# Scores on two row tiles of 64x128 in place of four 64x64 tiles

## The chip, the cores and the metric

The kernel runs on one core of a Trainium2 chip. The metric is the device time of that core in microseconds (us). Times of several runs are given by their median; a trace comes from one profiled execution.

## What is computed

A chunked linear attention with decay, followed by a mixture of experts with one expert for each token. There are 4 batches, 8 heads, 768 positions and a head size of 64; 3072 tokens of width 512; 8 experts with 1024 hidden units. Cut to what matters:

```
for each block of the sequence, for each batch and head:
    scores = (q_block @ k_block.T) * decay_mask        # lam ** (i - j), 0 above the diagonal
    out    = scores @ v_block + (q_block * lam ** (i + 1)) @ kv_state
    kv_state = lam ** block * kv_state + (k_block * rev_decay).T @ v_block
x = attention output, one row of 512 for each token
expert  = argmax(x @ w_gate + modality_bias);  gate = softmax value of that expert
result  = gate * (relu(x @ w1[expert]) @ w2[expert])
```

## The kernel before

Two stages follow one another. The attention stage works on 24 chunks of 128 positions (6 for each of 4 batches, `g` from 0 to 23), each with all 8 heads. Heads go in pairs: of the 128 partitions a pair's first head has 0 to 63 and its second 64 to 127. The second stage multiplies tiles of up to 256 tokens, gathered by expert, with that expert's weights in fp32r.

TensorE can be used as one array of 128 rows by 128 columns, or as several smaller tiles (64x64, 128x64 and so on) that stand in different rows or columns of it. The rows are those of the operands' partitions, the columns those of the output's partitions; the profile shows the shape in use for each group as "64*64", "128*64", "128*128". All attention matmuls are plain fp32.

One turn of the chunk loop (lines 721 to 775) gives TensorE, in this order:

- `scores(g)`, line 204: for each of 4 head pairs and each head (`hl`, its 64 partitions are the slice `r`), keys times queries, in two halves `s` of the 128 key positions. Each matmul has 64 rows (the head size), 64 weight columns (64 keys) and streams 128 queries: four 64x64 tiles, 16 matmuls for a chunk. The two heads write two PSUM tiles `s` of one bank each (chunk 1 uses a tile `x` for the second). VectorE multiplies each with the decay mask into `pt` (line 207).
- `from_state(g - 1)`, line 242: the carried state times decayed queries, on 64x64 tiles, into PSUM tiles `o`. It is left out for the first chunk of a batch.
- `outputs(g - 1)`, line 253: values times `pt` of the chunk before, on two 128x64 column tiles, added to the same `o`; ScalarE copies `o` to `xt` (line 255).
- `carry(g)`, line 219: what the chunk adds to the state, on two 128x64 column tiles; left out for the last chunk of a batch.
- `tokens(g - 2)`, line 266: turns `xt` to rows of tokens and adds the gate's logits, on two 128x64 column tiles.

The matmuls that rank the tokens for their experts (lines 321 to 326 and 360, 128x128) stand among these at a few places. SyncE's queue loads the chunks, 1 MB each, up to 6 ahead (line 73); ScalarE's queue writes the tokens out (line 270). The tile framework orders each engine's instructions by the program and adds the waits.

In the second stage line 572 transposes gathered tokens, and lines 579, 582 and 583 are the three fp32r products.

Of the kernel before, what the change touches and what calls it, by code (L numbers as in the profile page):

```python
# [37 lines left out]
def linear_attention_moe(tc, qkv, lam, modality, wg, mbias, w1, w2, out):  # L38
    nc = tc.nc
    with ExitStack() as ctx:  # L40
# [118 lines left out]
        halves2 = [slice(hl * D, (hl + 1) * D) for hl in range(2)]  # L159
# [8 lines left out]
        def loaded(g):  # L168

            t = chunks[g]  # L170
            kt, qt = (t[:, 0, i].rearrange("p (a t) -> p a t", a=NP) for i in range(2))
            return kt, qt, t[:, 1, 0], t[:, 1, 1]
# [23 lines left out]
        def scores(g):  # L196
            kt, qt, vt, kn = loaded(g)
            pts = []
            sps = [ps.tile([P, NP, P], F32, name="s", bufs=3),
                   ps.tile([P, NP, P], F32, name="x", bufs=2) if g == 1 else ps.tile([P, NP, P], F32, name="s", bufs=3)]  # L200
            for p in range(NP):
                for hl, r in enumerate(halves2):
                    for s in halves2:
                        nc.tensor.matmul(sps[hl][s, p, :], kt[r, p, s], qt[r, p, :], start=True, stop=True)  # L204
            for hl in range(2):
                pt = work.tile([P, NP, P], F32, name="pt", bufs=4)
                op = nc.vector.tensor_tensor(out=pt, in0=sps[hl], in1=dk[:, hl], op=ALU.mult)  # L207
                pts.append(pt)
            return pts, op
# [511 lines left out]
        for g in range(0, ng + 2):  # L721
            if g == 2:
                routing_constants()
            if g < ng:
                st1[g], masked = scores(g)
# [59 lines left out]
        hl = [work.tile([P, 2, TT], F32R, name=f"hl{i}", tag=t, bufs=3) for i, t in enumerate(("qd", "qd", "kd", "kd"))]  # L785
# [149 lines left out]
```

## Time and profile before

| | us |
|---|---|
| median of 3 runs | 414.44 (411.96 to 415.23) |
| profiled execution | 410.95 |
| its span, first to last instruction | 409.2 |
| TensorE busy with matmuls | 392.8 (96% of the span) |
| VectorE busy | 248.5 (61%) |
| ScalarE busy | 190.6 (47%) |
| GpSimd busy | 101.4 (25%) |

The profile has PE for TensorE's matmuls and PEld for its weight loads, which overlap them; DVE is VectorE, ACT ScalarE, POOL GpSimd, SP SyncE; a q behind an engine is its DMA queue. L204 is line 204. Matmuls are pipelined: one's busy time reaches into the next one's, so the pace of a group is read from starts, not from durations. The attention stage lies at about 6 to 108 us.

### The profile page before, as it was taken

Reading aid. Unit: us, or ns where it says so; the run is one execution under the profiler, and the core shown is the slowest. Engines: PE = TensorE matmul, PEld = TensorE weight load, DVE = VectorE, ACT = ScalarE, POOL = GpSimd, SP = SyncE. Lnnn points to the kernel's source line nnn. Section 1 sums busy time; section 2 is a strip of 40 time slices with the busy share of each in tenths; the row PEclk is TensorE's granted clock in tenths of the full one; section 3 lists DMA queues with packets and bytes.
Section 4 is the critical chain, followed back from the end, with each engine's and each line's share of the span. In section 5 each row is a group of like instructions: output and inputs, shape, how many; then the busy total and the mean of one; then the engine's idle time right before and its main releaser. Section 6 shows DMA issues by size and latency. Waiting matters only on the chain.

```text
span 409.2 us, 10757 instructions
## 1 busy us (share of the span) xinstructions
PE 392.8 (96%) x4224; PEld 347.7 (85%) x4224; DVE 248.5 (61%) x480; ACT 190.6 (47%) x345; POOL 101.4 (25%) x118
## 2 busy tenths in 40 slices
PE   8998989999799999999999999999999999999994
PEld 4877878888598987698999989898999989898983
DVE  6958849888489850378390918456381918366240
ACT  1333434443586231466463818274463818274330
POOL 4301323514513651041331210203021210200001
PEclk9999999999999999999999999999999999999999
DMA  7999979888820168010316586501111010200101
GB/s 284 408 384 409 352 277 343 284 293 286 314 79 3 53 192 332 11 54 1 105 50 217 172 276 203 185 33 51 53 51 54 23 55 26 70 28 7 48 1 48
DMA packets 24603, 62.58 MB, mean 153 GB/s; under 512 B 7645, under 2 KB 8157, under 8 KB 24544
## 3 DMA queue, kind: packets, MB, share of 16 engines
q1 hardware_dynamic: 15792, 42.81, 29.9%
q0 software_dynamic: 4768, 12.69, 9.3%
q10 hardware_dynamic: 3984, 6.31, 4.2%
q8 instruction: 35, 0.57, 0.5%
q14 instruction: 24, 0.20, 0.2%
HBM read 90.46 MB, written 13.67 MB: 254 GB/s over the span
## 4 chain that ended last, share of the span: by engine, by line
issue 45%; PE 26%; DMA 10%; POOL 7%; DVE 3%; POOLq 3%; SPq 3%; ACT 1%; DVEq 0%
PE s L204 6%; PE o L253 6%; PE x L266 6%; DMA idx<-inv 5%; POOL out_dram L657 4%; DMA xg<-xs,idx 4%; POOL xg L539 3%; POOLq L837 3%; PE o L242 2%; PE kv L219 2%; DMA load<-in_qkv_dram 2%; SPq L556 1%; DVE w1l L512 1%; PE s L583 1%; PE s L582 1%
## 5 line engine op out<-in xcount | busy, mean ns | idle before, releaser
L579 PE MATMUL s<-xh,w1h 128*128 128x256 f32 x384 | 107.4, 280 | 0.8 <-ACT xh L511 0.8
L583 PE MATMUL s<-xh,w1l 128*128 128x256 f32 x384 | 107.3, 280 | 0.5 <-DVE w1l L512 0.4
L582 PE MATMUL s<-xl,w1h 128*128 128x256 f32 x384 | 107.2, 279 | 0.0
L512 DVE TENSOR_TENSOR w1l<-raw,w1h 128x1024 fp32r<-128x1024 f32 x48 | 58.1, 1221 | 72.6 <-ACT w1h L511 72.6
L579 PE MATMUL o<-w2h,hh 128*128 128x512 f32 x192 | 75.8, 395 | 0.0
L583 PE MATMUL o<-w2h,hl 128*128 128x512 f32 x192 | 74.9, 390 | 0.0
L582 PE MATMUL o<-w2l,hh 128*128 128x512 f32 x192 | 74.8, 390 | 0.0
L579 PEld LDWEIGHTS s<-xh,w1h 128*128 128x128 f32 x384 | 72.2, 188 | 1.8 <-ACT xh L511 1.0
L583 PEld LDWEIGHTS s<-xh,w1l 128*128 128x128 f32 x384 | 72.2, 188 | 0.9 <-DVE w1l L512 0.9
L582 PEld LDWEIGHTS s<-xl,w1h 128*128 128x128 f32 x384 | 72.2, 188 | 0.6 <-issue 0.2
L512 DVE TENSOR_TENSOR w2l<-raw,w2h 128x1024 fp32r<-128x1024 f32 x48 | 58.5, 1220 | 2.1 <-ACT w2h L511 2.0
L511 ACT CAST w1h<-raw 128x1024 fp32r<-128x1024 f32 x48 | 49.8, 1055 | 20.4 <-PE s L582 19.7
L511 ACT CAST w2h<-raw 128x1024 fp32r<-128x1024 f32 x48 | 50.1, 1046 | 0.0
L656 ACT ACTIVATE y<-o,idx 128x512 f32<-128x512 f32 x20 | 13.8, 689 | 76.0 <-PE o L583 45.6
L657 POOL DMA_INDIRECT out_dram<-y,idx x20 | 20.3, 1013 | 115.5 <-ACT y L656 94.8
L598 DVE SCALAR_TENSOR_TENSOR hl<-s,hh 128x512 fp32r<-128x512 f32 x48 | 33.0, 688 | 21.6 <-ACT hh L597 21.5
L539 POOL DMA_INDIRECT xg<-xs,idx x20 | 25.3, 1264 | 73.6 <-PE x L572 68.0
L255 ACT COPY xt<-o 128x256 f32<-128x256 f32 x48 | 17.7, 373 | 54.0 <-PE o L253 49.1
L583 PEld LDWEIGHTS o<-w2h,hl 128*128 128x128 f32 x192 | 36.0, 188 | 7.5
L582 PEld LDWEIGHTS o<-w2l,hh 128*128 128x128 f32 x192 | 36.1, 188 | 7.2
L579 PEld LDWEIGHTS o<-w2h,hh 128*128 128x128 f32 x192 | 36.1, 188 | 7.1
L207 DVE TENSOR_TENSOR pt<-s,dk 128x512 f32<-128x512 f32 x47 | 30.1, 679 | 16.9 <-PE s L204 16.8
(185 smaller groups left out, 485.8 us busy)
## 6 DMA issues: line engine op xcount, KB each, us to landing
raw<-in_w_dram SPq DMA_DIRECT2D x104, 512.0 KB
load<-in_qkv_dram SPq DMA_DIRECT2D x22, 1024.0 KB
xs<-xn ACTq DMA_DIRECT2D x24, 256.0 KB
load<-in_qkv_dram SPq DMA_DIRECT2D x4, 512.0 KB
spare<-in_w_dram SPq DMA_DIRECT2D x4, 512.0 KB
w1h<-in_w_dram SPq DMA_DIRECT2D x4, 512.0 KB
inv<-pad SPq DMA_DIRECT2D x2, 196.0 KB
inv<-pad SPq DMA_DIRECT2D x2, 192.0 KB
```

What stands on the lines that cost most here:

```text
L204: nc.tensor.matmul(sps[hl][s, p, :], kt[r, p, s], qt[r, p, :], start=True, stop=True)
L207: op = nc.vector.tensor_tensor(out=pt, in0=sps[hl], in1=dk[:, hl], op=ALU.mult)
L253: mm = nc.tensor.matmul(op[half][place(p, hl), i, :], vt[:, (2 * p + hl) * D : (2 * p + hl + 1) * D], pts[hl][:, p, :], start=(c == 0 and ...
L266: nc.tensor.matmul(xp[r, j, : P + E], xt[:, p, r], iw[:, p, :], start=True, stop=True)
L511: cp = nc.scalar.copy(out=hi, in_=src)
L512: df = nc.vector.tensor_tensor(out=lo, in0=src, in1=hi.bitcast(F32), op=ALU.subtract)
L539: last = nc.gpsimd.indirect_dma_start(out=(to or xg)[t][:m], out_offset=None, in_=xs[:rows, :], in_offset=bass.IndirectOffsetOnAxis(ap=idx ...
L579: mm = nc.tensor.matmul(out, ah, bh, start=first, stop=False)
L582: nc.tensor.matmul(out, ah, bl, start=False, stop=False)
L583: return nc.tensor.matmul(out, al, bh, start=False, stop=last)
L598: nc.vector.scalar_tensor_tensor(out=hl[i], in0=hp, scalar=0.0, in1=hh[i].bitcast(F32), op0=ALU.max, op1=ALU.subtract)
L657: sc = nc.gpsimd.indirect_dma_start(out=out, out_offset=bass.IndirectOffsetOnAxis(ap=idx[:, t, 0:1], axis=0), in_=y, in_offset=None, bound ...
```

## The change

The four 64x64 tiles of the scores become two row tiles of 64x128: one matmul takes all 128 keys of a head as its 128 weight columns. There are 8 matmuls for a chunk in place of 16, each with the same 64 rows and 128 streamed queries. The PSUM tiles, what is written into them, and all other lines stay.

```diff
@@ -200,8 +200,7 @@
             for p in range(NP):
                 for hl, r in enumerate(halves2):
-                    for s in halves2:
-                        nc.tensor.matmul(sps[hl][s, p, :], kt[r, p, s], qt[r, p, :], start=True, stop=True)
+                    nc.tensor.matmul(sps[hl][:, p, :], kt[r, p, :], qt[r, p, :], start=True, stop=True)
             for hl in range(2):
```

## Rows read from the trace of the kernel before

**Rows 1.** Stretches: length; busy time (count) by engine; granted clock, DMA share, GB/s.

```profile
11.70:51.00 39.30, 37.36 (x863) 32.56 (x865) 32.26 (x82) 14.64 (x54) 7.00 (x11) 1.00 1.01 387
...
115.00:409.00 294.00, 287.36 (x1983) 258.59 (x1981) 162.60 (x244) 146.54 (x193) 62.73 (x54) 1.00 0.26 85
```

**Rows 2.** Chain of waits, 11.7 to 108.3 us, shares of that window by line.

```profile
by line: PE s L204 26.3%; PE o L253 25.0%; PE x L266 22.3%; PE o L242 9.8%; PE kv L219 9.3%; issue 5.9%; PE x L321 0.4%; ACT xn L268 0.4%; PE x L326 0.3%; PE x L360 0.1%; PE x L324 0.1%; ACT xe L269 0.1%
```

**Rows 3.** Groups by shape: tile, operands, count; busy us, mean ns; idle before.

```profile
L204 PE MATMUL s<-load 64*64 64x128 f32 x752 | 29.7, 277 | 2.9 <-issue 2.1 <-DMA load<-in_qkv_dram 0.8
...
L242 PE MATMUL o<-qd,state 64*64 64x128 f32 x320 | 14.0, 271 | 0.2 <-issue 0.2
```

**Rows 4.** TensorE in order of time: start us, length us, group, count; clean chunks.

```profile
60.46 1.10 PE L204 MATMUL s<-load 64*64 64x128 f32 x32
61.49 1.09 PE L253 MATMUL o<-pt,load 128*64 128x128 f32 x16
62.41 0.64 PE L219 MATMUL kv<-load,kd 128*64 128x64 f32 x16
62.88 1.10 PE L266 MATMUL x<-iw,xt 128*64 128x136 f32 x16
63.91 1.10 PE L204 MATMUL s<-load 64*64 64x128 f32 x32
64.83 0.62 PE L242 MATMUL o<-qd,state 64*64 64x128 f32 x16
65.38 1.09 PE L253 MATMUL o<-pt,load 128*64 128x128 f32 x16
66.30 0.63 PE L219 MATMUL kv<-load,kd 128*64 128x64 f32 x16
```

**Rows 5.** TensorE in order of time, the last chunk, which has no scores.

```profile
105.63 0.67 PE L242 MATMUL o<-qd,state 64*64 64x128 f32 x16
106.23 1.09 PE L253 MATMUL o<-pt,load 128*64 128x128 f32 x16
```

**Rows 6.** TensorE in order of time: transposes (one, then three), fp32r matmuls.

```profile
108.34 0.33 PE L572 MATMUL x<-ident,xg 128*128 128x128 f32 x1
...
108.34 0.55 PE L572 MATMUL x<-ident,xg 128*128 128x128 f32 x3
...
113.27 0.39 PE L579 MATMUL s<-xh,w1h 128*128 128x256 f32 x1
113.49 0.28 PE L582 MATMUL s<-xl,w1h 128*128 128x256 f32 x1
113.61 0.28 PE L583 MATMUL s<-xh,w1l 128*128 128x256 f32 x1
```

**Rows 7.** TensorE in order of time: first and last of seven gapped bursts.

```profile
26.11 0.66 PE L253 MATMUL o<-pt,load 128*64 128x128 f32 x8
27.50 0.66 PE L253 MATMUL o<-pt,load 128*64 128x128 f32 x8 [0.73 <-issue]
27.99 1.10 PE L266 MATMUL x<-iw,xt 128*64 128x136 f32 x16
...
102.05 0.62 PE L242 MATMUL o<-qd,state 64*64 64x128 f32 x16
103.68 1.09 PE L253 MATMUL o<-pt,load 128*64 128x128 f32 x16 [1.01 <-issue]
```

**Rows 8.** Stretches of about 256 TensorE instructions, columns as in the first group.

```profile
33.55:39.96 6.41, 5.45 (x127) 4.67 (x127) 5.43 (x13) 1.64 (x6) 0.94 (x2) 1.00 1.04 408
...
45.40:53.37 7.97, 6.05 (x128) 5.07 (x126) 4.89 (x14) 2.53 (x10) 2.77 (x3) 1.00 0.94 323
53.37:58.53 5.16, 5.16 (x126) 4.63 (x128) 2.83 (x6) 1.64 (x6) 0.96 (x1) 1.00 0.53 195
...
64.08:69.33 5.25, 5.04 (x135) 4.44 (x131) 4.63 (x14) 2.03 (x8) 2.71 (x4) 1.00 0.96 307
```

**Rows 9.** The page: busy time and instructions of engines; DMA queue of instructions: packets, MB, share.

```profile
PE 392.8 (96%) x4224; PEld 347.7 (85%) x4224; DVE 248.5 (61%) x480; ACT 190.6 (47%) x345; POOL 101.4 (25%) x118
...
q8 instruction: 35, 0.57, 0.5%
```

## What was predicted, before the change was run

> **What bounds the kernel now.** I read the stretches first [rows 1]. From 11.7 to 51 us TensorE is busy for 37.4 of 39.3 us with the DMA share at 1.01; from 115 us on it is busy for 287 of 294 us. So TensorE sets the pace in both stages, and a microsecond taken from or given to its attention stage should arrive at the end nearly whole. The chain of waits over 11.7 to 108.3 us says the same [rows 2]: the five groups of attention matmuls hold 93% of it, 5.9% is "issue" (TensorE waits for nothing that the profile shows), and no DMA or VectorE work holds 1%. So I looked for two things only: how long TensorE's bursts are, and where those issue gaps come from.
>
> The bursts are regular [rows 4]; I read them from the start of one burst to the start of the next. A chunk with a carried state is scores 0.92 us (63.91 to 64.83), state part 0.55 (64.83 to 65.38), outputs 0.92 (65.38 to 66.30), carry 0.47 (as 62.41 to 62.88), tokens 1.03 (62.88 to 63.91): 3.89 us.
>
> What does a score burst consist of? The trace shows each fp32 matmul as two, so the 16 of a chunk stand as 32 [rows 4]. The granted clock is 1.00 in both stretches, the 2.4 GHz level [rows 1], so durations compare. A lone pass of 128 columns with the whole array as one tile takes 0.11 us: three transposes last 0.22 us longer than one [rows 6]. The outputs, on two column tiles, do 16 passes in 0.92 us; the scores, on four tiles, do 32 in the same 0.92 us [rows 4]. So four passes run side by side in the scores: eight rounds of 0.109 us make 0.87, and 0.05 stays for the first weight load.
>
> **The change, part by part.**
>
> *Passes.* Half as many passes run two at a time: 16 on two row tiles are again eight rounds, 0.87 us. The row halves already run side by side in four tiles, so I price the streaming at nothing gained, nothing lost. No row shows 64x128 tiles side by side; if they ran one after the other it would be 16 rounds, a rival below.
>
> *A new change of shape.* Now scores and state part share 64x64, and the state part follows without a break. When another shape follows the scores, as in a batch's first chunk (60.46 to 61.49), the burst takes 1.03 in place of 0.92: 0.11 to change. A state part that follows another shape takes 0.60 (105.63 to 106.23 [rows 5]) and not 0.55: its first weight load is no longer hidden, 0.05. So 0.16 us for each score burst followed by a state part. There are 320/16 = 20 state bursts [rows 3], of which the one at 105.63 already follows other work: 19 x 0.16 = 3.0 us. The changes tokens to scores (128x64 to 64x64 now, 128x64 to 64x128 then) and state part to outputs exist on both sides. Bounds: 0 if 64x128 to 64x64 were no change of shape, 3.0 if it is one. Every row with a change of row or column size pays, so I take 3.0.
>
> The Trainium skill, "TensorEngine Tiling (Array Packing)", section "Tiling Modes", says that changing the tiling mode, other than changing the tile within it, drains TensorE. The trace agrees where 64x64 turns into 128x64 (0.11 us); by this rule the new change pays too, and the term stays 3.0.
>
> *Wider weight loads.* A score weight grows from 64 to 128 columns. The load ahead of the first round is exposed. Lower bound: 0.05, as for 64 columns. Upper bound: an fp32r matmul with 128 weight columns takes 0.22 us first in its burst and 0.12 after (113.27 to 113.49 to 113.61 [rows 6]), so 0.10. It is the nearest row, four-byte data of the same width: I take 0.10, 0.05 more for 24 bursts, 1.2 us (bounds 0 and 1.2).
>
> In steady rounds the load must hide behind one pass of the same 128 columns. The carry has that ratio, 64 weight columns to 64 streamed ones: eight rounds in 0.47 us are 0.058 each, against 0.0545 for half of 0.109. That is 0.004 a round: 24 x 8 x 0.004 = 0.8 us. Lower bound 0; upper bound from the fp32r row (0.117 by its steady step of 0.12, 0.008 over 0.109): 1.5 us.
>
> Added: 3.0 + 1.2 + 0.8 = 5.0 us, bounds 3.0 and 5.7.
>
> *Fewer instructions.* Seven bursts hold an issue gap. The first [rows 7] takes 1.88 us in place of 0.92 (26.11 to 27.99), the last 1.63 in place of 0.55 (102.05 to 103.68). By such differences the seven, in order, lose 0.96, 0.64, 1.19, 2.3, 0.54, 0.89 and 1.08 us, 7.6 in all. What are they waiting for? I cut the stage at the ends of the gaps, and between them where a count of about 256 falls, and counted TensorE's matmuls and weight loads [rows 8]: 254, 254, 254 and 266 in the windows shown (a window also counts what runs across its edges), between 252 and 271 in all 15 from 16 to 103.7 us. The seven gaps stand at the ends of such windows. So the gaps fall on a grid of about 256 instructions. The queue of kind "instruction" [rows 9] carries 35 packets, 0.57 MB, so 16 KB each, and TensorE has 4224 matmuls and 4224 loads [rows 9]: 241 for each packet. I conclude that TensorE's instructions come in packets of 256 and that it sometimes runs dry because the next one is late behind the data transfers: the DMA share is 1.04, 0.94 and 0.96 in the stalled windows shown, and 0.53 in one that has no gap.
>
> In a stalled window TensorE used up its packet and waited, so the window's length is how long the next packet took: 5.25 us at the shortest, 6.41 and 7.97 at the longest. A packet now lasts 256/192 x 3.89 = 5.2 us without a gap, since a chunk has 2 x (32+16+16+16+16) = 192 instructions. After the change a chunk has 160 and takes 3.89 + 0.16 + 0.05 + 0.03 = 4.13 us: 256/160 x 4.13 = 6.6 us. Six of the seven late packets would then be in time, and the slowest leaves 1.4 us: 7.6 - 1.4 = 6.2 us gained. This assumes that a packet is asked for about when the previous one is begun. If it is asked for halfway, only 0.7 of the 1.4 us more counts, and 0.3 + 0.5 + 1.6 + 0.2 + 0.4 = 3.0 stays: 4.6 gained. Bounds 0 (a rival) and 7.6; I take 6.2.
>
> The Trainium skill, "Runtime: NRT & Kernel Launch", section "Instruction fetch mechanics", says that instructions are refilled in blocks of 256 and that crossing a block is mostly hidden. The block size agrees with the windows, the hiding doesn't (up to 2.3 us lost at one). By the page's word on hiding the gaps would be something else, and fewer instructions would gain nothing: the sum would be 5.0 us slower.
>
> *Other engines.* The products with the decays (L207) still wait for the last score pass of the chunk, which ends where it did; no wait is added and no tile or buffer changes. The input chunks aren't on the chain, so a slightly faster or slower TensorE meets them in time.
>
> *Sum.* +5.0 - 6.2 = -1.2 us. Against the profiled execution (410.95 us, of which the span is 409.2) that is 409.8. The median of the runs shown, 414.44, lies 3.5 above the profiled one; on it the forecast is 413.2, rounded 413. The three runs spread over 3.3 us; if late packets cause that spread the gain is larger, which I leave to the range.
>
> **Rivals.**
>
> *Nothing is saved* (the other side). The gaps stay, because they don't come from the number of instructions, or because the packets take longer by as much. For it: that packets are asked for early is inferred. Against it: the grid of 256 that the gaps keep to. The page's "mostly hidden", of the Trainium skill's "Runtime: NRT & Kernel Launch" above, would make it this case. Price +5.0 (3.0 to 5.7): 419.4 us (417.4 to 420.1). It decides from a saving under 0.9 us on: then the change is slower by over 1% with the added work at 5.0.
>
> *The row tiles run one after the other.* 24 bursts x 8 rounds x 0.109 = 21 us more; the longer bursts leave time for all late packets, -7.6, and 5.0 stays: +18, 433 us. For it: no row has this shape in pairs, and a load of the full width might block the other tile. Against it: with four tiles, loads and passes of both row halves overlap fully.
>
> *The new shape change is free or the wider loads are*, and the packets come in time: added work 0 to 2 us, gain 6.2 or more (also where other runs stall more than the profiled one did): -4.2 to -7.6, about 409 us. Against it: every shape change in the rows pays its 0.1.
>
> **Chances.** My sum, with its own range -4.6 to +1.1 us (added 3.0 to 5.7, gained 4.6 to 7.6, so 410 to 415.5): 0.6. Nothing saved: 0.17. One after the other: 0.07. Free or larger gain: 0.16. About 1%, 4.1 us, is what a measurement of this kernel can tell from no change: faster takes the last case and the edge of mine, 0.19; slower takes 0.07 and most of the 0.17, 0.19; the same is 0.62. The range reaches to 420 to take in the second case and down to 408.5 into the last; it leaves out the serial tiles and the largest gains.
>
> **What would show it.** In the new trace the scores should stand as 384 matmuls on 64*128; scores to state part about 1.1 us and state part to outputs 0.60; the instruction queue some 32 packets; issue gaps on TensorE with one or two left, so that issue on the chain from 11.7 us on falls under 2%. A state part that still follows in 0.92 refutes the shape term; a burst of 1.9 us means serial tiles; issue gaps of 5 us or more in sum refute the saving.

## The result, and the profile after

| | before | after |
|---|---|---|
| median of 4 runs, us | 414.59 (411.96 to 415.23) | 407.57 (407.28 to 408.68) |
| ratio after to before | | 0.9864, 95% interval 0.9824 to 0.9903 |
| span of the profiled execution, us | 409.2 | 405.9 |
| first scores of chunk 2 to first transposes (L572, L571 after), us | 96.61 | 92.74 |
| start of the first transposes to start of the last matmul, us | 294.59 | 294.79 |

By the medians the changed kernel is 7.0 us (1.7%) faster; by the ratio in the table, which isn't the quotient of the two medians, it is 1.4%. The forecast was 413.0, and 407.6 lies 0.9 us below the low end of the range. The second stage is the same within 0.2 us. The two profiled executions (410.95 and 407.58 us) differ by 3.4 us: the attention stage gained 3.87, and a later start of chunk 2 (12.05 us in place of 11.73) and the second stage took 0.5 of it back. The other 3.6 us of the medians' difference come from the executions of before that weren't profiled, and they are a part of the story.

The page of the kernel after, which answers to [rows 9], and its group of score matmuls, which answers to the first of [rows 3] (tile shape, operands, count; busy us, mean ns; idle before):

```profile
PE 395.4 (97%) x3840; PEld 349.8 (86%) x3840; DVE 248.6 (61%) x480; ACT 190.6 (47%) x345; POOL 99.4 (24%) x118
...
q8 instruction: 32, 0.52, 0.5%
...
L203 PE MATMUL s<-load 64*128 64x128 f32 x376 | 30.1, 286 | 0.7 <-DMA load<-in_qkv_dram 0.7
```

TensorE has 384 matmuls and 384 weight loads fewer, and the queue of instructions three packets fewer. The scores' group is busy for 30.1 us, where it had 29.7, and has no idle time that ended by "issue"; before it had 2.1 us of it.

The chain of waits of the kernel after, 12.05 to 80 us, and then that of the kernel before from 11.7 to 80 us, shares by line:

```profile
by line: PE s L203 29.5%; PE o L252 24.8%; PE x L265 21.9%; PE o L241 13.2%; PE kv L218 9.8%; PE x L320 0.4%; PE x L325 0.3%; PE x L359 0.2%; PE x L323 0.1%; issue 0.1%
```

```profile
by line: PE s L204 27.6%; PE o L253 24.7%; PE x L266 21.3%; PE o L242 9.8%; PE kv L219 9.7%; issue 6.0%; PE x L321 0.4%; PE x L326 0.3%; PE x L360 0.2%; PE x L324 0.1%
```

"Issue" has gone from 6.0% to 0.1%. The scores and the state part (L241) have grown, from 37% to 43% of a shorter chain. So the change took away idle time that was nobody's work, and paid for it with longer bursts.

The bursts, in the timeline of TensorE after (start us, length us, group, count), to be read against [rows 4]:

```profile
63.77 1.10 PE L265 MATMUL x<-iw,xt 128*64 128x136 f32 x16
64.80 1.16 PE L203 MATMUL s<-load 64*128 64x128 f32 x16
65.89 0.67 PE L241 MATMUL o<-qd,state 64*64 64x128 f32 x16
66.49 1.09 PE L252 MATMUL o<-pt,load 128*64 128x128 f32 x16
67.41 0.64 PE L218 MATMUL kv<-load,kd 128*64 128x64 f32 x16
```

From start to start the scores take 1.09 us (64.80 to 65.89) where they took 0.92, the state part 0.60 (to 66.49) where it took 0.55. Outputs (0.92), carry (0.47) and tokens (1.03) are as they were. Of the score burst itself the first round, with its exposed weight load, takes 0.213 us where it took 0.160, and a later round 0.112 where it took 0.109.

The stretches of after, with busy time (count) by engine, granted clock, DMA share and GB/s, answer to [rows 1]:

```profile
12.05:51.00 38.95, 38.95 (x743) 34.31 (x743) 32.48 (x83) 14.85 (x55) 7.33 (x11) 1.00 1.02 395
...
112.00:406.00 294.00, 287.01 (x1978) 258.24 (x1977) 162.37 (x242) 145.96 (x193) 61.61 (x54) 1.00 0.26 85
```

TensorE is busy for all 38.95 us of the first stretch, beside a DMA share as high as before.

### The profile page after: what moved, and what is told of

It is laid out like the page before. It is cut to its first block, busy times and chain, and to the rows that moved or that the text cites. A ratio compares the mean times of both kernels' runs of the same rounds, so it can differ in the third digit from the quotient of the medians.

```text
span 405.9 us, 9991 instructions
## 1 busy us (share of the span) xinstructions
PE 395.4 (97%) x3840; PEld 349.8 (86%) x3840; DVE 248.6 (61%) x480; ACT 190.6 (47%) x345; POOL 99.4 (24%) x118
## 3 DMA queue, kind: packets, MB, share of 16 engines
q1 hardware_dynamic: 15792, 42.81, 30.1%
## 4 chain that ended last, share of the span: by engine, by line
issue 44%; PE 20%; DMA 16%; POOL 8%; DVE 3%; SPq 3%; POOLq 3%; ACT 0%; DVEq 0%
PE s L203 5%; DMA load<-in_qkv_dram 5%; DMA idx<-inv 4%; PE o L252 4%; POOL out_dram L656 4%; PE x L265 4%; DMA raw<-in_w_dram 4%; DMA xg<-xs,idx 4%; POOL xg L538 3%; POOLq L836 3%; PE o L241 2%; PE kv L218 2%; SPq L555 1%; DVE w1l L511 1%; PE s L582 1%
## 5 line engine op out<-in xcount | busy, mean ns | idle before, releaser
L538 POOL DMA_INDIRECT xg<-xs,idx x20 | 24.0, 1202 | 73.4 <-PE x L571 68.0
L206 DVE TENSOR_TENSOR pt<-s,dk 128x512 f32<-128x512 f32 x47 | 30.1, 679 | 14.0 <-PE s L203 14.0
```

The source lines that it names most:

```text
L538: last = nc.gpsimd.indirect_dma_start(out=(to or xg)[t][:m], out_offset=None, in_=xs[:rows, :], in_offset=bass.IndirectOffsetOnAxis(ap=idx ...
```

## The experiments

The theory: TensorE's instructions arrive in packets of 256; while the chunks are being loaded a packet takes 5 to 8 us, and TensorE runs dry when it uses one up sooner. Fewer instructions for each chunk make a packet last longer. The first rival: the gaps have to do with 64x64 tiles, and a shape that has none of them in the scores has no gaps. The second: the gaps come and go with the execution, and the after that was seen was a lucky one.

"Time of a packet" below is 256 divided by TensorE's instructions for a chunk, times the time of a chunk without gaps. A gap is counted from start to next start of TensorE's matmuls and loads, less what such a step usually takes; it is "on the grid" if it falls within one instruction of every 256th. Counted so, the seven gaps of the profile before are 6.6 us. (The prediction counted whole bursts and had 7.6: each restart costs about 0.14 us more, for a weight load that is exposed again.)

### The kernel before a second time

No edit.

> The kernel before, unchanged, with a second profile. If the spread of its runs (412 to 415 us) comes from late instruction packets, this profile shows issue gaps at the same grid of 256 TensorE instructions but of another sum than 7.6 us, and its span differs from 409.2 us by about the difference of the sums. If the spread comes from elsewhere, the sum stays near 7.6 us and the stretch after 108 us differs.

Measured: 414.51 us, 3.6 above the execution profiled first; in the other runs of before that went with it the median was 412.19. The stage takes 98.63 us (12.18 to 110.81) where it took 96.61. The chain of waits of this execution, 12.2 to 110.8 us, by line:

```profile
by line: PE s L204 25.9%; PE o L253 24.5%; PE x L266 21.9%; PE o L242 9.7%; PE kv L219 9.1%; issue 7.8%; ACT xn L268 0.4%; PE x L321 0.4%; PE x L326 0.3%; PE x L360 0.1%; ACT xe L269 0.1%; PE x L324 0.1%
```

Issue is 7.8% where [rows 2] had 5.9%: ten gaps on the grid, 8.9 us. One of them, in the timeline of TensorE, begins within the same burst as the first of [rows 7] and is longer (1.56 us in place of 0.73):

```profile
26.62 0.66 PE L253 MATMUL o<-pt,load 128*64 128x128 f32 x8
28.84 0.66 PE L253 MATMUL o<-pt,load 128*64 128x128 f32 x8 [1.56 <-issue]
```

Of the rest of the 3.6 us, some 0.45 lies ahead of the stage (chunk 2 starts at 12.18 us in place of 11.73) and 1.2 behind it, in the stretch of 8 us after the first transposes (columns as above), first of this execution and then of the one profiled before the change:

```profile
110.80:118.80 8.00, 6.22 (x40) 5.06 (x41) 4.72 (x11) 5.49 (x12) 4.93 (x5) 0.79 0.39 116
```

```profile
108.30:116.30 8.00, 6.12 (x50) 4.94 (x50) 4.94 (x12) 5.74 (x12) 4.95 (x5) 1.00 0.51 161
```

The granted clock is 0.79 in place of 1.00: for a part of the stretch the fp32r matmuls start 0.21 us apart and not 0.12, which is the level of 1.2 GHz. That costs 1.2 us. So two executions of the kernel before differ by their gaps (2.3 us on the grid), and by this stretch; the execution that I took the sum from had fewer gaps than this one, and no slow stretch.

### Both kernels without the later loads

```diff
-    load_chunk(g + LOADS - 1)
+    chunks[g + LOADS - 1] = chunks[g - 1]
```

The chunks after the sixth aren't loaded; the first six are used again. The same edit in both kernels.

> The kernel before without the chunk loads after the first six: later chunks read the first six again (so the output is another one, and the second stage may have another number of tiles). Late packets behind the data transfers: the issue gaps of 0.4 us and more vanish, and the attention stage from the scores of chunk 2 to the first transposes shrinks from 96.6 to about 89 us, though its instructions and tiles are those of before. Gaps that belong to the four-tile shape itself: they stay, about 7 us, and the stage stays at 96 us.

> The changed kernel without the chunk loads after the first six, as in the run before it (the output is another one). It has no gaps to lose: its attention stage should stay at 92.7 us under both theories. If late packets are the cause, it is then some 4 us slower in this stage than the kernel before without loads (19 state parts at 0.22 us, and 5 other bursts at 0.06 us), which is the bare cost of the new shape.

Other tokens go to other experts then, and the second stage gets one more tile: only the attention stage compares. It takes 91.11 us in the kernel before (11.70 to 102.81) and 92.79 in the one after (12.35 to 105.14). The chains of that stage, before and then after:

```profile
by line: PE s L204 27.3%; PE o L253 25.9%; PE x L266 23.0%; PE o L242 10.1%; PE kv L219 9.9%; issue 2.4%; ACT xn L268 0.8%; PE x L321 0.4%; PE x L326 0.4%; PE x L360 0.1%; PE x L324 0.1%; ACT xe L269 0.1%
```

```profile
by line: PE s L203 27.9%; PE o L252 25.4%; PE x L265 22.5%; PE o L241 12.9%; PE kv L218 9.8%; ACT xn L267 0.8%; PE x L320 0.4%; PE x L325 0.4%; PE x L359 0.1%; PE x L323 0.1%; ACT xe L268 0.1%; issue 0.0%
```

Without the loads the order turns round: the old shape is faster, by 1.6 us from chunk 3's scores on (86.25 against 87.87), though it still has three gaps on the grid (at 22.3, 92.3 and 98.2 us, 2.5 to 2.9 us). Without those the new shape would be 4.1 to 4.5 us slower: that is its bare price. The kernel before gains 5.5 us in that stretch when the loads go (91.76 to 86.25), the one after none (87.82 to 87.87): the loads cost the one kernel time through its gaps and the other nothing. That three gaps were left is a miss of 2 us for what I expected of the first. They stand where the DMA engines were still full. Three stretches of the kernel before without the later loads (columns as above):

```profile
13.00:21.00 8.00, 8.00 (x198) 7.29 (x202) 8.00 (x20) 3.25 (x12) 1.59 (x3) 1.00 1.03 380
30.00:60.00 30.00, 30.00 (x722) 26.95 (x715) 26.20 (x66) 13.15 (x49) 8.44 (x10) 1.00 0.20 74
90.00:98.20 8.20, 6.89 (x165) 5.80 (x162) 6.55 (x17) 2.53 (x10) 4.47 (x5) 1.00 1.03 410
```

The first gap stands at the end of the first stretch, while the first loads still come in; the other two are in the third, in which the second stage's weights do (`raw`, 512 KB each). From 30 to 60 us the DMA share is 0.20, and TensorE is busy for 30.00 of 30 us. So it isn't the chunk loads as such: here packets were late where other transfers filled the DMA engines, whichever these were.

### Kernel after, outputs cut in two

Back to 192 instructions for a chunk, with the scores on row tiles: if the gaps go with the count, they come back; if with the shape, not.

```diff
-                    mm = nc.tensor.matmul(op[half][place(p, hl), i, :], vt[...], pts[hl][:, p, :], start=(c == 0 and i == 0), stop=(i == NP // 2 - 1))
+                    for s in halves2:
+                        mm = nc.tensor.matmul(op[half][place(p, hl), i, s], vt[...], pts[hl][:, p, s], start=(c == 0 and i == 0 and s.start == 0), stop=(i == NP // 2 - 1 and s.stop == P))
```

> The changed kernel with each output matmul (L252) cut in two of 64 streamed columns: same shape and work, but 32 more TensorE instructions for a chunk, so 192 again. The cut alone costs some 0.06 us for a chunk (16 rounds at 0.058 in place of 8 at 0.109), 1.5 us. Late packets: a packet lasts 5.5 us again, gaps come back with some 4 to 6 us, about 413 us. Gaps tied to the four-tile shape: none come back, about 409 us.

Measured: 414.74 us, 1.0086 (1.0052 to 1.0120) of the kernel before in the same comparison, so all of the gain was lost. But it was lost otherwise than expected. The timeline of TensorE:

```profile
61.26 1.25 PE L253 MATMUL o<-pt,load 128*64 128x64 f32 x32
62.29 0.69 PE L218 MATMUL kv<-load,kd 128*64 128x64 f32 x16
```

The cut outputs take 1.03 us where they took 0.92, and the tokens 1.08 where they took 1.03: 0.16 us for each chunk, 3.8 in all, of which I had expected 1.5. There is only one gap on the grid, 1.35 us, where I expected 4 to 6. The edit that was to raise the count made the chunks longer as well, and a packet lasts 5.7 us in place of the 5.2 of the kernel before. This run alone doesn't tell count from shape; it suggests that the time of a packet matters, and not the number of packets (35, as before).

### Old shape with slower tokens, new shape with more instructions

So the two were crossed. First the kernel before with the same number of instructions, but longer ones: the tokens' weights are widened with zeros, and each of their matmuls streams 256 columns in place of 136.

```diff
-    iw: [P, NP, P + E]
+    iw: [P, NP, 2 * P], zero but for wg in iw[:, :, P : P + E]
-    nc.tensor.matmul(xp[r, j, : P + E], xt[:, p, r], iw[:, p, : P + E], ...)
+    nc.tensor.matmul(xp[r, j, :], xt[:, p, r], iw[:, p, :], ...)
```

> The kernel before (four 64x64 tiles, 192 TensorE instructions for a chunk) with the token matmuls (L267) streaming 256 columns in place of 136, the further ones multiplied by zeros: the same instructions, but a chunk lasts 4.67 us in place of 3.89 and a packet of 256 instructions 6.2 us in place of 5.2. Late packets: the gaps go from 7.6 us to 2 at most, as in the changed kernel, and the stage from chunk 2 to the first transposes takes 96.6 - 7.6 + 24 x 0.78 = 108 to 110 us. Gaps tied to the four-tile shape: they stay at about 7 us, 115 us.

Then the kernel after with outputs cut as above and the tokens cut too: 224 instructions for a chunk, more than the kernel before has.

```diff
-    nc.tensor.matmul(xp[r, j, :], xt[:, p, r], iw[:, p, :], ...)
+    for s in (slice(0, P // 2), slice(P // 2, P + E)):
+        nc.tensor.matmul(xp[r, j, s], xt[:, p, r], iw[:, p, s], ...)
```

> The changed kernel (row tiles of 64x128) with the output matmuls and the token matmuls each cut in two along the streamed columns: 224 TensorE instructions for a chunk of about 4.4 us, so that a packet lasts 5.0 us, less than before the change. Late packets: gaps come back in the row-tile shape, 7 us or more in sum, and the stage takes about 105 us or more. Gaps tied to the four-tile shape: one gap or none, as with 192 instructions, and 99 to 100 us.

Measured, slower tokens: 425.17 us, stage 109.9. Its stretch from 13 to 75 us (columns as above):

```profile
13.00:75.00 62.00, 62.00 (x1260) 48.87 (x1257) 45.25 (x116) 22.11 (x82) 13.12 (x17) 1.00 0.94 343
```

TensorE is busy for 62.00 of 62 us: on 64x64 tiles, with 192 instructions for a chunk and as many packets as before (35), and no gap on the grid. A packet lasts 6.2 us here.

Measured, more instructions: 433.11 us, stage 114.8, nine gaps on the grid, 11.5 us. Four stretches of it between one end of a packet and the next:

```profile
22.31:29.36 7.05, 5.46 (x127) 4.81 (x127) 4.37 (x9) 1.64 (x6) 0.00 (x0) 1.00 0.95 355
29.36:35.09 5.73, 5.25 (x127) 4.62 (x127) 2.01 (x5) 2.01 (x7) 0.00 (x0) 1.00 1.01 359
35.09:40.12 5.03, 4.96 (x129) 4.61 (x128) 3.04 (x7) 2.01 (x7) 0.62 (x1) 1.00 1.03 341
40.12:46.46 6.34, 5.11 (x127) 4.59 (x128) 6.24 (x17) 2.08 (x8) 1.23 (x2) 1.00 0.97 341
```

Each holds 254 to 257 matmuls and loads, and TensorE is idle in three of them, for 0.5 to 1.6 us. The gap at the end of the first, in the timeline:

```profile
27.32 0.45 PE L241 MATMUL o<-qd,state 64*64 64x128 f32 x8
29.36 0.45 PE L241 MATMUL o<-qd,state 64*64 64x128 f32 x8 [1.59 <-issue]
```

These two refute the rival of the shape: old tiles without a gap, new ones with more gaps than the kernel before has.

### Kernel before, outputs cut in two

The same cut as in the kernel after, now with the old scores: 224 instructions for a chunk and the shortest packets, 4.6 us.

> The kernel before (four 64x64 tiles) with each output matmul cut in two of 64 streamed columns: 224 TensorE instructions for a chunk of some 4.0 us, a packet of 256 lasts 4.6 us. Late packets: more gaps on the grid than before (6.6 and 8.9 us in its two profiles) and than the row tiles with 224 instructions (11.5 us at 5.0 us a packet): 12 us or more, so 420 us or more (before plus 3.9 us for the cut plus 4 us or more). If the number of instructions doesn't matter: before plus 3.9 us.

Measured: 431.56 us, stage 114.3, nine gaps on the grid, 12.9 us, the most of all. One of them:

```profile
40.83 0.45 PE L254 MATMUL o<-pt,load 128*64 128x64 f32 x6
43.70 1.54 PE L254 MATMUL o<-pt,load 128*64 128x64 f32 x26 [2.43 <-issue]
```

The stage's length isn't the price of its gaps alone. From 30.41 to 33.83 and from 44.06 to 47.48 us, just behind two of the gaps, the granted clock is 0.50, and there are pauses off the grid at about 85 to 94 us. The first of the two stretches (columns as above):

```profile
30.41:33.83 3.42, 3.42 (x60) 2.78 (x57) 1.08 (x2) 0.45 (x2) 0.00 (x0) 0.50 0.86 319
```

### A mix of both shapes

If a packet need only last long enough, perhaps half of the chunks can keep the cheaper four tiles: row tiles in the even chunks, four tiles in the odd ones, 176 instructions on average.

```diff
-    for s in halves2:
+    for s in (halves2 if g % 2 else [slice(0, P)]):
```

> The row tiles on chunks with even g, the four 64x64 tiles on those with odd g: 176 instructions for a chunk on average, a packet of about 5.8 us; 8 state parts pay the change of shape in place of 19, so 2.4 us less than the changed kernel without gaps. Late packets: one or two gaps, the time within 2 us of the changed kernel (some 406 to 410 us where that one has 407.6). Gaps tied to the four-tile shape: half of them stay, about 4 us, and it ends 1 to 2 us above the changed kernel.

> The mixed kernel once more, beside the changed kernel. A state part follows row-tile scores in 11 chunks in place of 19, so without gaps it should be 8 x 0.22 = 1.8 us below the changed kernel; its profile had 0.5 us of gaps on the grid, so 1 to 2 us below is expected if the pauses off the grid, seen in every profile of the second call, belonged to that chip. If they belong to this kernel it is again some 3 us above.

Measured, in two comparisons: 416.57 us, 0.9946 (0.9907 to 0.9984) of the kernel before, and 414.86 us, 0.9900 (0.9863 to 0.9938). In both it is behind the changed kernel, by 3.2 and 2.4 us, where I expected it within 2 us and then 1 to 2 us ahead. On the grid it lost 0.5 and 1.4 us. The larger part lies elsewhere, in the stretch from 74 us on:

```profile
74.00:111.30 37.30, 33.92 (x648) 28.23 (x644) 23.79 (x78) 13.71 (x52) 13.25 (x16) 1.00 0.80 279
```

TensorE is idle for 3.4 us in it, most of it in pauses that don't stand on the grid; the changed kernel that was run beside it idles for 1.9 us there (34.60 us, 32.71 busy). The mix isn't better; why it has more of these pauses stays open.

### Both kernels again

No edits. The two of the kernel after stood beside the runs above, to see whether it is always without gaps; the third profile of the kernel before is from a later run by itself.

> The changed kernel again, on the chip and beside the runs of before of this call. Late packets that vary from run to run: its runs spread less than those of before, and its profile has no gap of a packet; the ratio to before stays at 0.985 to 0.99. If the first comparison caught slow runs of before, the ratio moves to 0.99 to 1.00.

> The changed kernel a third time, as the measure for the mixed kernel: ratio to before 0.985 to 0.990 (so far 0.986 and 0.990), no gap on the grid in its profile.

> The kernel before once more, for a third profile. Late packets: 6 to 9 us of gaps on the grid of 256, as in its two earlier profiles. If the chip is one of those where the runs of before take about 419 us, some pauses off the grid at about 75 to 85 and 102 to 106 us are expected too, as in all profiles from there; if the run is at 412 to 415 us, none.

| comparison | before | after | ratio (95%) |
|---|---|---|---|
| first | 414.59 | 407.57 | 0.9864 (0.9824 to 0.9903) |
| second | 418.78 | 413.35 | 0.9897 (0.9862 to 0.9933) |
| third | 419.13 | 412.44 | 0.9842 (0.9800 to 0.9883) |

The gain came three times, 5.4 to 7.0 us. Neither of the two new profiles of the changed kernel has a gap on the grid; the third profile of the kernel before has seven, 5.5 us. From 13 to about 75 us, first the kernel after (second comparison), then the kernel before (its third profile):

```profile
13.00:74.00 61.00, 61.00 (x1160) 53.90 (x1158) 50.14 (x129) 24.04 (x88) 14.86 (x19) 1.00 1.00 370
```

```profile
13.00:75.00 62.00, 57.95 (x1349) 50.89 (x1346) 49.31 (x127) 23.38 (x87) 14.29 (x19) 1.00 0.97 359
```

No idle time in the one, 4.05 us in the other. The stage takes 103.07 us in that third profile of the kernel before (418.65 us) and 96.54 in the profile of the kernel after from the third comparison (412.56 us). These 6.5 us aren't the price of the gaps on the grid: the two ran on different chips (3 and 10 in the record), the kernel before has some 2.3 us more of the pauses described next, and from 108.18 to 111.60 us, inside its stage, its granted clock is 0.50.

Both kernels are 4 to 6 us slower in these two comparisons than in the first. What they have there, and what no profile of the first comparison has, are pauses off the grid, such as these in the third profile of the kernel before:

```profile
78.83 0.55 PE L242 MATMUL o<-qd,state 64*64 64x128 f32 x8
79.69 0.45 PE L242 MATMUL o<-qd,state 64*64 64x128 f32 x3 [0.31 <-issue]
80.43 0.46 PE L242 MATMUL o<-qd,state 64*64 64x128 f32 x4 [0.30 <-issue]
```

They lie at about 75 to 86 and 101 to 109 us, about 0.7 us apart, with a few matmuls between, and take 4.65 us in this profile and 2.3 to 2.4 in those of the kernel after. Every profile from chips 3, 9 and 10 has such pauses, whatever the kernel, and none from chip 6 or from the first comparison. So they aren't the change's doing; their cause wasn't settled.

### All profiles in one table

| kernel | scores | instructions a chunk | time of a packet, us | gaps on the grid, us (count) |
|---|---|---|---|---|
| before, outputs cut | 64x64 | 224 | 4.6 | 12.9 (9) |
| after, outputs and tokens cut | 64x128 | 224 | 5.0 | 11.5 (9) |
| before, three profiles | 64x64 | 192 | 5.2 | 6.6 (7), 8.9 (10), 5.5 (7) |
| before, later loads left out | 64x64 | 192 | 5.2 | 2.5 (3) |
| after, outputs cut | 64x128 | 192 | 5.7 | 1.35 (1) |
| mix, two profiles | both | 176 | 5.8 | 0.5 (1), 1.4 (3) |
| before, slower tokens | 64x64 | 192 | 6.2 | 0 |
| after, three profiles | 64x128 | 160 | 6.6 | 0, 0, 0 |
| after, later loads left out | 64x128 | 160 | 6.6 | 0 |

While the chunks are loaded, the loss falls with the time of a packet (profiles of one kernel differ by up to 3.4 us), whichever shape the scores have and however many instructions a chunk has. From 6.2 us on nothing is left.

What TensorE waited for stands in the traces themselves, which hold the start and the length of every 16 KB packet of the instruction queue. Five crossings from one packet of 256 to the next (us):

| kernel | last start in the old packet | last 16 KB transfer that ended before the next start | next start |
|---|---|---|---|
| before | 26.50 | 25.26 to 26.14 | 27.50 |
| before | 51.18 | 51.04 to 52.01 | 53.37 |
| before | 58.53 | 55.27 to 56.26 | 58.53 |
| before, outputs cut | 41.05 | 41.32 to 42.28 | 43.70 |
| after | 72.54 | 67.97 to 70.53 | 72.54 |

The stages of all 14 traces have 52 pauses over 0.2 us on the grid (the 50 of the table of profiles, and two small ones of the first profile before), and each of them ends 1.21 to 1.62 us after such a transfer. In the three profiles of the kernel after, from 14 us on, every transfer had ended at least 2.0 us before TensorE came to the crossing. So the gaps are waits for these transfers: this is read from the traces, and doesn't rest on the count of 256 alone.

## Why the prediction was partly right

**The bound** held. TensorE sets the pace of both stages: what the attention stage gained came out at the end, and the second stage moved by 0.2 us (294.59 and 294.79 us).

**Passes** held: two row tiles run side by side, a later round takes 0.112 us. The rival of serial tiles, 433 us, is out.

**The change of shape** held: the score burst is 0.17 us and the state part 0.05 us longer. The wider first load and the rounds are in that 0.17; take their 0.053 and 7 x 0.0025 away, and 0.10 stays for the change, 0.15 with the state part's 0.05, where 0.16 was predicted. 19 x (0.168 + 0.051) is 4.2 us, and the other bursts of the stage add 0.2. (In the working, the burst at 60.46 was called a batch's first chunk. It is the chunk after one; the state part that is left out there is the first chunk's, which comes a turn late. The count of 19 stands.) The rule of the Trainium skill, "TensorEngine Tiling (Array Packing)", section "Tiling Modes", that a change of mode drains TensorE, agrees with the trace for this pair of shapes too.

**Wider loads** held: the first round pays 0.053 us more (predicted 0.05), the later ones 0.0025 each (predicted 0.004). In sum the added work is 4.4 us where 5.0 was forecast, and the pair without loads says 4.1 to 4.5 by another way.

**Fewer instructions** is where the sum failed: the mechanism was right, its size wasn't. I took 6.2 us; between the two profiled executions it was 4.4 + 3.9 = 8.3. Two steps of it fell:

- *The slowest packet leaves 1.4 us.* It left nothing; neither did any other in three profiles. I took each packet's duration in the stalled kernel as a fixed time that the new kernel would meet as well. The traces show that it isn't. From TensorE's entry into one packet to the end of the next one's transfer it took 3.8 to 6.6 us ahead of the seven gaps, and 1.25 to 4.83 us in the three profiles of the kernel after; with at most 1.62 us from there to a start that is 6.5 us, inside the 6.6 of a packet. The cut outputs say the same: with a packet lasting 5.7 us, durations of 5.25 to 7.97 us would leave six gaps and about 4.4 us, and one of 1.35 was seen. The other half of the step, that a packet is asked for about when the previous one is begun, fits: in both kernels without the later loads, from 30 to 85 us, the transfers start between 0.6 us before and 1.7 us after that moment. What wasn't fixed is how long they wait while the DMA engines are full; why they waited less in the new kernel isn't shown. Two small stalls of about 0.2 us each, at 21.4 and 45.4 us, which I hadn't counted, went as well. With the 7.6 of the seven they make 8.0; the last 0.3 of the 8.3 I can't place.
- *The gaps of one execution stand for all.* The profiled execution (410.95 us) is faster than each of the four timed ones. The second profile of the kernel before, 414.51 us, which is close to their median, loses 2.3 us more at the grid and 1.2 us to the slow stretch behind the stage. Against that one the changed kernel's stage is 5.9 us shorter (98.63 to 92.74), and with the slow stretch that makes 7.1, where the difference of the medians is 7.0. That the two agree so well is partly luck: this profile belongs to runs whose median was 412.19, and what the four timed executions of the first comparison lost isn't on record. I had written that a larger gain follows if late packets cause the spread of the runs, and left it to the range, which then ended at 408.5. The spread of 3.3 us was a hint, though no proof, since the kernel after, with no gap on the grid in its profiles, spread over 4.0 us in the third comparison (410.53 to 414.57): a term that is a sum of stalls differs from run to run, and what removes it gains, at the median, what the median run loses, not what the profiled one does.

So the likeliest case, no change within 1%, didn't come; faster by more than that had been given 0.19. What came is its own sum with a saving larger than its upper bound of 7.6. It is nearest to the last rival by its size, but not by its ground, since neither the change of shape nor the load was free.

**Nothing saved** is refuted by the stalls' going, by three comparisons, and by the tables. The rule that had stood for it, that the crossing of a block of 256 is mostly hidden (the Trainium skill, "Runtime: NRT & Kernel Launch", section "Instruction fetch mechanics"), is true here where a packet lasts 6.2 us and more and false below: 5.5 to 12.9 us are lost at 4.6 to 5.2, and 0.5 to 1.4 at 5.7 and 5.8.

**What would show it.** The 384 matmuls on 64*128 (376 as one group, the rest into another tile), 1.09 and 0.60 us, 32 packets and issue under 2% (0.1) all came as written; "one or two gaps left" didn't.

## What to carry to other kernels

If TensorE stands idle at "issue" while the DMA engines are full, count its matmuls and loads between the gaps: if 256 come out, and a transfer of the instruction queue ends shortly before each restart (1.2 to 1.6 us here), what it waits for are its own instructions, and fewer of them help where no faster operation would. Longer ones end the waiting too, but cost more than they gained here (425.17 us with slower tokens, beside 418.78). A change of tile shape that costs 0.15 us in each burst can then be the cheaper choice. And a term that is a sum of stalls wants more than one execution, or the median of the runs beside the profiled time, before it is put into a sum.

## What the runs showed of the hardware

- Instructions late for TensorE: gaps of up to 2.8 us that stand at multiples of 256 instructions, and end 1.21 to 1.62 us after a 16 KB transfer of the instruction queue. It takes full DMA engines (the windows of the seven gaps of the first profile before have mean shares of 0.76 to 1.04) and short packets: with the later loads left out the same kernel lost 2.5 us in place of 5.5 to 8.9, and with packets of 6.2 us and more none was seen at shares of 0.94 to 1.02. The share alone doesn't decide: at 58.53:64.08 of that profile it is 1.02, and there is no gap.
- The price of narrower streams: outputs of 64 columns in place of 128, in twice as many matmuls of the same columns in all, took 1.03 us in place of 0.92.
- TensorE can fall to half clock behind the attention stage, and inside it. The timeline of the second profile of the kernel before has an idle wait ahead of it and then steps of 0.21 us:

```profile
114.08 0.68 PE L266 MATMUL x<-iw,xt 128*64 128x136 f32 x8 [0.99 <-DVE xl L512]
...
117.01 0.41 PE L582 MATMUL s<-xl,w1h 128*128 128x256 f32 x1
117.22 0.41 PE L583 MATMUL s<-xh,w1l 128*128 128x256 f32 x1
...
119.03 0.28 PE L583 MATMUL s<-xh,w1l 128*128 128x256 f32 x1
119.14 0.28 PE L579 MATMUL s<-xh,w1h 128*128 128x256 f32 x1
```

  Ahead of it TensorE had been idle for 0.77 and 0.99 us. The first profile of the kernel before has the same two idle times (0.78 and 0.99 us) and no such stretch (1.00 in the 8 us behind the stage), so they alone don't bring it about. Two of the three profiles of the kernel after have one behind the stage (0.79 from 108.60 to 115.00 us in the last). Others lie inside the stage, after gaps or pauses: in the kernel before with its outputs cut (two, above), in the third profile of the kernel before (0.82 from 105.50 to 115.00 us), and in the second of the kernel after (0.50 from 77.53 to 80.94 us). In the profile shown it costs 1.2 us; neither kernel is free of it, and what brings it about wasn't tried.
- The pauses off the grid: in the profiles of the second and third comparison and in the third profile of the kernel before, in old and new shape alike; open.
